# Three stages instead of four over the features of the first two token blocks, in a fused recurrence and cosine-gated feed-forward kernel

## The chip, the cores and the metric

The kernel runs on one core of a Trainium2 chip. The metric is the device time of one execution in microseconds (us). Before the change the median of three runs is 477.37 us (477.19 to 477.85). About 0.2% (0.95 us) is what a measurement of this kernel can tell from no change.

The engines are named as the profile names them: PE (TensorE, matmuls), PEld (its weight loads), DVE (VectorE), ACT (ScalarE), POOL (GpSimd) and SP (SyncE, whose queue issues nearly all DMAs).

## What is computed

```python
# r, k, v: (4, 8, 768, 48) float32; w, u: (8, 48)
for t in range(S):                       # a recurrence over 768 positions
    cur = einsum('bhd,bhe->bhde', u * k[t], v[t])
    y[t] = einsum('bhd,bhde->bhe', r[t], state + cur)
    state = w * state + einsum('bhd,bhe->bhde', k[t], v[t])
x = y.transpose(0, 2, 1, 3).reshape(3072, 384)
h = x @ w_in                             # w_in: (384, 2048), float64 in memory
out = ((h * cos(h)) @ w_out).astype(float32)   # w_out: (2048, 384), float64
```

## The kernel before, in words

**Attention.** The recurrence is computed in 24 chunks of 128 token rows. The first 8 (`chunk`, L1006) and the other 16 (`late_chunk`, `late_slot`, L1323 to L1633) use different loads and layouts, but each ends in a PSUM bank that holds 128 columns of x in three pieces of 128 features. ACT rounds that bank to the high half xh and DVE subtracts it to get the low half xl (L1233 and L1242 for the first 8 chunks, L1622 and L1627 in `split` for the late ones). For a late chunk the PSUM bank (`xp`) comes from the same ring of three banks (`B_H`) in which the feed-forward's products h are formed.

**Feed-forward.** The 24 chunks make six blocks of four chunks (512 token columns). The 2048 features are 16 groups of 128. One step is one block with one group: h takes 9 matmuls of 128x512 (three pieces of the 384 inputs times the three products high-high, low-high and high-low; `mm_h`, L553); then ACT and DVE take five passes over it (L571 whole turns, L574 the rest, L577 the sine table, L1733 the product with h, L1736 high half, L1739 low half); then 9 matmuls of 128x512 (`mm_ot`, L566) add the group's share to three accumulators in PSUM banks 0 to 2. The last block does its second product in the other orientation (`mm_o`, L559). PE is allowed to run the second product some steps after the first.

**Weights.** They lie in DRAM as float64. Each group has two pieces, one of w_in and one of w_out. A piece is loaded to a tile `raw` (ring of three, shared with the late chunks' loads), turned into float32 by integer operations (L934 on ACT, L942 and L954 on DVE, L963 an addition on POOL or DVE), rounded to a high half (L975 on ACT or L978 on DVE) and subtracted to a low half (L966 on DVE or POOL). `conv` (L906 to L983) writes these operations; the subtraction is `o8`. Of `conv(i)`, i = 2f is the w_in piece of group f and i = 2f+1 its w_out piece. They are converted once, and stay.

**Stages.** The weights come in slower than PE could use them if block 0 took all 16 groups first. So blocks 0 and 1 (`GRP = 2`) take turns: `CUTS` cuts the 16 groups into stages, block 0 takes a stage's groups, then block 1 takes the same ones, then the next stage begins. Blocks 2 to 5 take all groups in one go. With cuts at 0, 2, 5, 10 and 16 the 32 steps of the first two blocks need a new group at steps 0 and 1, 4 to 6, 10 to 14, and 20 to 25; in the steps between them block 1 uses groups that are there. At each turn the three accumulators are copied out of PSUM to an SBUF tile (L1787, the tile names are `ot`, `ztu` and `s`) and, when that block's next stage begins, copied back (L1766). All these copies run through two lambdas, L1760 on ACT and L1761 on DVE. The second products of the new stage wait for the copy back.

**The order.** Nothing runs in the order in which the program writes it. Each instruction group is an `Op` with an engine, a cost, a latency `lat` and a due time; `Plan.one_pass` (L427) is a list scheduler that picks, engine by engine, the operation that is ready with the earliest due time. It works with these numbers alone, before anything runs. The due times stand in the table `DUES` (one entry per operation, in nanoseconds), with `HOLDS` (how long an engine may be held for a more urgent operation) and `ALTS` (which of two engines an operation takes). `lat` is added to an operation's end both for the operations that depend on it and for the moment at which a buffer is free again:

```python
t = max(t, max(o.end + o.lat for o in x.owner.users))      # _free_at
t = max((d.end + d.lat for d in o.after), default=0.0)     # _ready
```

Once placed, each engine's queue is fixed: on the chip an engine waits at its next instruction even if a later one is ready. All first products are in the order of the steps (`line="h"`), and so are all second products (`line="o"`). Until the first h, PE's planned gaps are filled with dummy matmuls (`warm_up`, L1865).

Of the kernel before, what the change touches and what calls it, by code (L numbers as in the profile page):

```python
# [29 lines left out]
CUTS = (0, 2, 5, 10, 16)  # L30
# [285 lines left out]
}  # L316
ALTS = {
# [3 lines left out]
}  # L321
# [162 lines left out]
def kernel(  # L484
# [11 lines left out]
    nc = tc.nc  # L496
# [1526 lines left out]
```

## Time and profile before

| what | us |
|---|---|
| median of three runs | 477.37 |
| the profiled execution's own time | 478.65 |
| its span, first to last instruction | 476.8 |
| PE busy in the span | 468.6 (98%) |
| DVE busy | 366.2 (77%) |
| ACT busy | 303.1 (64%) |
| POOL busy | 212.8 (45%) |

The profiled execution's own time is 1.85 us longer than its span and 1.28 us longer than the median. TensorE's granted clock is 0.999 of full speed over the span. A view by windows gives the busy time of each engine in a stretch. A timeline row gives start, length, engine, line, operation, output and inputs; in brackets stands the idle time of that engine just before and what ended it. Matmul durations overlap: the pace of PE is read from the starts.

### The profile page before, as it was taken

What the parts mean: (1) busy time and instruction counts of PE and PEld (TensorE: products, weight loads), DVE (VectorE), ACT (ScalarE), POOL (GpSimd) and SP (SyncE); (2) the same over time, 40 slices, a digit from 0 to 9 for tenths busy, and PEclk for the clock granted to TensorE, in tenths of its full rate; (3) what the DMA queues carried; (4) which work ended last, traced back from release to release, by engine and by line L of the source; (5) the groups of instructions that cost most, each with busy time, mean ns of one, the idle gap of its engine ahead of it and who ended that gap; (6) DMA issues with size and microseconds to landing.
All of it is one profiled execution on the core that took longest, in us unless ns stands there. A gap on an engine that the chain in (4) does not pass through costs nothing.

```text
span 476.8 us, 11745 instructions
## 1 busy us (share of the span) xinstructions
PE 468.6 (98%) x4480; PEld 391.5 (82%) x4480; DVE 366.2 (77%) x679; ACT 303.1 (64%) x667; POOL 212.8 (45%) x217
## 2 busy tenths in 40 slices
PE   8899999999999999999999999999999999999996
PEld 7788888888878888788888888888888888898996
DVE  7998999999998877868887878776857666655552
ACT  5988978877877546465556556657547556344453
POOL 6865537536557786537864337543344200000000
PEclk9999999999999999999999999999999999999999
DMA  7883555437257646478646357644448300020001
GB/s 151 185 204 104 161 128 146 134 93 177 73 148 154 133 104 131 117 154 183 160 122 158 108 122 200 151 137 96 122 122 199 99 28 0 17 50 2 1 1 70
DMA packets 139233, 55.39 MB, mean 116 GB/s; under 512 B 122244, under 2 KB 135076, under 8 KB 139172
## 3 DMA queue, kind: packets, MB, share of 16 engines
q1 hardware_dynamic: 138964, 54.35, 47.0%
q8 instruction: 36, 0.59, 0.5%
q14 instruction: 25, 0.20, 0.1%
q10 hardware_dynamic: 208, 0.25, 0.1%
HBM read 49.86 MB, written 4.72 MB: 114 GB/s over the span
## 4 chain that ended last, share of the span: by engine, by line
PE 90%; DVE 3%; ACT 2%; POOL 2%; issue 1%; SPq 1%; DMA 1%; POOLq 0%; DVEq 0%
PE bank L553 39%; PE bank L566 33%; PE bank L559 7%; PE bank L1605 3%; PE bank L1521 3%; ACT A L1116 1%; PE bank L1143 1%; PE bank L1178 1%; DMA f<-in_r_dram 1%; PE bank L1212 0%; POOL A L1502 0%; PE bank L1051 0%; DVE f L574 0%; SPq L1374 0%; ACT qi L571 0%
## 5 line engine op out<-in xcount | busy, mean ns | idle before, releaser
L553 PE MATMUL bank<-xh,w_in_hi 128*128 128x512 f32 x288 | 112.7, 391 | 0.7 <-DVE xl L1627 0.7
L553 PE MATMUL bank<-xh,w_in_lo 128*128 128x512 f32 x288 | 112.4, 390 | 0.2 <-DVE w_in_lo L966 0.2
L553 PE MATMUL bank<-xl,w_in_hi 128*128 128x512 f32 x288 | 112.2, 390 | 0.0
L574 DVE SCALAR_TENSOR_TENSOR f<-bank,qi 128x512 f32<-128x512 f32 (+1 forms) x102 | 66.5, 654 | 46.1 <-ACT qi L571 45.9
L571 ACT ACTIVATE qi<-bank 128x512 int32<-128x512 f32 (+1 forms) x102 | 58.1, 574 | 64.3 <-PE bank L553 63.0
L566 PE MATMUL bank<-gh,w_out_hi 128*128 128x512 f32 x240 | 95.0, 396 | 0.0
L566 PE MATMUL bank<-gl,w_out_hi 128*128 128x512 f32 x240 | 93.5, 389 | 0.0
L566 PE MATMUL bank<-gh,w_out_lo 128*128 128x512 f32 x240 | 93.4, 389 | 0.0
L577 ACT ACTIVATE f<-f 128x512 f32<-128x512 f32 (+1 forms) x102 | 61.5, 607 | 36.6 <-DVE f L574 33.4
L1733 DVE TENSOR_TENSOR bank<-bank,f 128x512 f32<-128x512 f32 x94 | 64.9, 693 | 18.1 <-ACT f L577 16.4
L1736 ACT CAST gh<-bank 128x512 fp32r<-128x512 f32 x94 | 54.9, 585 | 36.8 <-PE bank L566 24.0
L1739 DVE TENSOR_TENSOR gl<-bank,gh 128x512 fp32r<-128x512 f32 x94 | 64.3, 684 | 15.8 <-ACT gh L1736 15.1
L553 PEld LDWEIGHTS bank<-xh,w_in_hi 128*128 128x128 f32 x288 | 54.1, 188 | 12.2 <-DVE xl L1627 1.1
L553 PEld LDWEIGHTS bank<-xh,w_in_lo 128*128 128x128 f32 x288 | 54.0, 188 | 11.9 <-DVE w_in_lo L966 0.6
L553 PEld LDWEIGHTS bank<-xl,w_in_hi 128*128 128x128 f32 x288 | 54.1, 188 | 10.9
L1460 POOL TENSOR_TENSOR A<-rT,decT_r 48x512 f32<-48x512 f32 x30 | 38.9, 1297 | 36.0 <-PE bank L1605 28.0
L566 PEld LDWEIGHTS bank<-gh,w_out_hi 128*128 128x128 f32 x240 | 45.0, 188 | 9.7
L566 PEld LDWEIGHTS bank<-gh,w_out_lo 128*128 128x128 f32 x240 | 45.0, 188 | 9.4
L566 PEld LDWEIGHTS bank<-gl,w_out_hi 128*128 128x128 f32 x240 | 45.1, 188 | 8.9
L963 POOL TENSOR_TENSOR f<-f,raw 128x384 int32<-128x384 int32 x24 | 26.1, 1090 | 40.6 <-DVE f L954 17.3
L1502 POOL TENSOR_TENSOR A<-ident,a 64x512 f32<-64x512 f32 x32 | 35.3, 1102 | 16.0 <-DVE a L1494 9.3
L1444 POOL TENSOR_TENSOR kT<-kT,decT_k 112x512 f32<-112x512 f32 x15 | 19.5, 1297 | 30.8 <-DVE kT L1429 25.5
(154 smaller groups left out, 726.2 us busy)
## 6 DMA issues: line engine op xcount, KB each, us to landing
raw<-in_moe_w_in_dram SPq DMA_DIRECT2D x29, 384.0 KB
raw<-in_moe_w_out_dram SPq DMA_DIRECT2D x29, 384.0 KB
raw<-in_k_dram SPq DMA_DIRECT2D x63, 80.0 KB
raw<-in_r_dram SPq DMA_DIRECT2D x63, 80.0 KB
out_dram<-ot SPq DMA_DIRECT2D x80, 48.0 KB
k<-in_k_dram SPq DMA_DIRECT2D x32, 96.0 KB
f<-in_r_dram SPq DMA_DIRECT2D x32, 96.0 KB
vr<-in_v_dram SPq DMA_DIRECT2D x32, 96.0 KB
```

Of the source, the lines that this page charges most:

```text
L553: nc.tensor.matmul(ph, a, b_, start=(i == 0), stop=(i == len(mm) - 1))
L559: nc.tensor.matmul(acc, a[:, ts], b_[:, f, :], start=(first and i == 0), stop=(last and i == 2))
L566: nc.tensor.matmul(acc, b_[:, f, n * P : (n + 1) * P], a, start=(first and i == 0), stop=(last and i == 2), skip_group_check=True)
L571: nc.scalar.activation(qi, ph, AF.Copy, scale=INV_2PI, bias=0.25)
L574: nc.vector.scalar_tensor_tensor(q, ph, INV_2PI, qi, op0=ALU.mult, op1=ALU.subtract)
L577: nc.scalar.activation(q, q, AF.Sin, scale=TWO_PI, bias=0.5 * math.pi)
L963: return lambda: eng.tensor_tensor(ai(), ai(), cn(), op=ALU.add)
L1460: nc.gpsimd.tensor_tensor(by_batch(plane(ar, j))[rows[j]], by_batch(late_t(rT))[rows[j]], late_d(decT_r)[rows[j]], op=ALU.mult)
L1502: nc.gpsimd.tensor_tensor(plane(ar, j)[side[j]], ident2[side[j], None, :].to_broadcast(to), ab()[side[j], :, None].to_broadcast(to), op=AL ...
L1733: nc.vector.tensor_tensor(g()[:, cs], ph()[:, cs], q()[:, cs], op=ALU.mult)
L1736: nc.scalar.copy(gh()[:, cs], g()[:, cs])
L1739: nc.vector.tensor_tensor(gl()[:, cs], g()[:, cs], f32(gh())[:, cs], op=ALU.subtract)
```

## The change

Blocks 0 and 1 take the groups in three stages of 2, 5 and 9 instead of four of 2, 3, 5 and 6. Two latencies that the scheduler reckons with are raised: that of a conversion's last subtraction, from 0.2 to 0.8 us for groups 8 to 15, and that of the late chunks' xl, from 0.2 to 1.0 us. All three tables are new.

```diff
-CUTS = (0, 2, 5, 10, 16)
+CUTS = (0, 2, 7, 16)
...
             o8 = op(
-                DVE, due - 0.8, 0.58, rest_of(nc.vector), [o7], [ca], port=True, alts=[(POOL, 1.15, rest_of(nc.gpsimd), True)]
+                DVE, due - 0.8, 0.58, rest_of(nc.vector), [o7], [ca], lat=0.2 if i < 16 else 0.8, port=True, alts=[(POOL, 1.15, rest_of(nc.gpsimd), True)]
             )
...
                     lambda: nc.vector.tensor_tensor(xo_(1), xv(), f32(xo_(0)), op=ALU.subtract),
                     [x_h],
                     [xp, xbuf],
+                    lat=1.0,
                 )
```

The cores of the tables: `DUES` has 2005 entries instead of 2017. Its first 56 entries (0 to 55, operations of the start-up and of the first chunks) are the same; from entry 56 on nearly all differ, in part because 12 operations are gone and the later ones move up. `HOLDS` has 1423 entries instead of 1220, and `ALTS` 33 in both:

```diff
-    26: 1, 44: 1, 132: 1, 137: 1, 143: 1, 156: 1, 615: 1, 629: 1, 636: 1, 641: 1, 648: 1, 657: 1, 676: 1, 677:
-    1, 685: 1, 690: 1, 720: 1, 740: 1, 741: 1, 753: 1, 767: 1, 783: 1, 788: 1, 804: 1, 811: 1, 823: 1, 825: 1,
-    869: 1, 915: 1, 941: 1, 999: 1, 2000: 1, 2010: 1,
+    26: 1, 44: 1, 132: 1, 137: 1, 143: 1, 156: 1, 615: 1, 629: 1, 636: 1, 641: 1, 648: 1, 657: 1, 684: 1, 690:
+    1, 720: 1, 747: 1, 748: 1, 762: 1, 767: 1, 781: 1, 788: 1, 790: 1, 797: 1, 802: 1, 810: 1, 811: 1, 825: 1,
+    869: 1, 939: 1, 981: 1, 1091: 1, 1993: 1, 1998: 1,
```

With cuts at 0, 2, 7 and 16 a new group is needed at steps 0 and 1, 4 to 8, and 14 to 22.

## Rows read from the trace of the kernel before

**Rows 1.** The page's head and its first part: busy time by engine.

```profile
span 476.8 us, 11745 instructions
PE 468.6 (98%) x4480; PEld 391.5 (82%) x4480; DVE 366.2 (77%) x679; ACT 303.1 (64%) x667; POOL 212.8 (45%) x217
```

**Rows 2.** Busy time by windows; the first row names the columns.

```profile
core 0: us, PE busy (x) PEld busy (x) DVE busy (x) ACT busy (x) POOL busy (x), PEclk, DMA share, GB/s
0.00:10.00 10.00, 8.59 (x79) 6.92 (x81) 6.57 (x24) 5.29 (x11) 6.34 (x24) 1.00 0.81 161
10.00:20.00 10.00, 8.76 (x160) 7.09 (x160) 9.58 (x18) 9.20 (x30) 9.04 (x10) 1.00 0.84 182
...
30.00:40.00 10.00, 9.43 (x216) 8.07 (x210) 9.30 (x19) 9.83 (x28) 6.76 (x8) 1.00 0.57 160
...
56.00:64.00 8.00, 8.00 (x37) 6.62 (x36) 7.13 (x15) 7.37 (x16) 4.39 (x4) 1.00 0.56 147
...
130.00:140.00 10.00, 9.85 (x44) 7.84 (x43) 9.71 (x20) 8.50 (x18) 4.47 (x4) 1.00 0.50 137
...
200.00:210.00 10.00, 9.32 (x42) 7.39 (x41) 6.27 (x10) 4.42 (x11) 6.72 (x6) 1.00 0.77 165
...
470.00:477.00 7.00, 2.69 (x16) 2.32 (x15) 0.42 (x2) 0.96 (x2) 0.00 (x0) 0.95 0.28 102
```

**Rows 3.** PE's timeline: its three waits after the first 20 us.

```profile
36.26 1.16 PE L1143 MATMUL bank<-rT,kT 48*128 48x128 f32 x16 [0.54 <-ACT kT L1093]
...
135.90 0.50 PE L553 MATMUL bank<-xh,w_in_lo 128*128 128x512 f32 x1 [0.15 <-DVE w_in_lo L966]
...
202.29 0.50 PE L553 MATMUL bank<-xh,w_in_hi 128*128 128x512 f32 x1 [0.68 <-DVE xl L1627]
```

**Rows 4.** Lines 1760 and 1761: accumulator copies, ns min/median/max.

```profile
L1760 ACT COPY bank<-ot x9: 580/596/622, 63.6 to 132.2; 128x512 f32<-128x512 f32 x9
...
L1761 DVE COPY s<-bank x2: 685/689/693, 63.7 to 87.0; 128x512 f32<-128x512 f32 x2
```

**Rows 5.** DVE's passes per step (busy us, mean ns) and per weight piece (min/median/max).

```profile
L1733 DVE TENSOR_TENSOR bank<-bank,f 128x512 f32<-128x512 f32 x94 | 64.9, 693 | 18.1 <-ACT f L577 16.4
L574 DVE SCALAR_TENSOR_TENSOR f<-bank,qi 128x512 f32<-128x512 f32 x94 | 64.5, 686 | 43.5 <-ACT qi L571 43.2
L1739 DVE TENSOR_TENSOR gl<-bank,gh 128x512 fp32r<-128x512 f32 x94 | 64.3, 684 | 15.8 <-ACT gh L1736 15.1
...
L942 DVE TENSOR_SCALAR f<-raw x32: 342/354/1219, 16.7 to 150.1; 128x384 int32<-128x384 int32 x32
...
L954 DVE SCALAR_TENSOR_TENSOR f<-raw,f x32: 532/551/1262, 20.4 to 151.2; 128x384 int32<-128x384 int32 x32
...
L966 DVE TENSOR_TENSOR w_in_lo<-f,w_in_hi x13: 517/551/1380, 25.5 to 142.8; 128x384 fp32r<-128x384 f32 x13
```

**Rows 6.** PE's timeline: first matmuls of steps 6, 7 and 8, and a second product.

```profile
60.09 0.39 PE L553 MATMUL bank<-xh,w_in_hi 128*128 128x512 f32 x1
...
62.13 0.39 PE L566 MATMUL bank<-gh,w_out_hi 128*128 128x512 f32 x1
...
64.17 0.39 PE L553 MATMUL bank<-xh,w_in_hi 128*128 128x512 f32 x1
...
70.29 0.39 PE L553 MATMUL bank<-xh,w_in_hi 128*128 128x512 f32 x1
```

**Rows 7.** DVE's and POOL's timelines, 58 to 70 us: conversions of groups 4 and 5.

```profile
58.16 0.55 DVE L966 TENSOR_TENSOR w_in_lo<-f,w_in_hi 128x384 fp32r<-128x384 f32 x1
...
65.89 0.70 DVE L1429 STREAM_TRANSPOSE kT<-raw 128x512 f32<-128x512 f32 x1
...
68.27 1.02 POOL L966 TENSOR_TENSOR w_out_lo<-f,w_out_hi 128x384 fp32r<-128x384 f32 x1 [0.29 <-ACT w_out_hi L975]
...
68.39 1.12 DVE L942 TENSOR_SCALAR f<-raw 128x384 int32<-128x384 int32 x1
69.43 0.55 DVE L966 TENSOR_TENSOR w_in_lo<-f,w_in_hi 128x384 fp32r<-128x384 f32 x1
```

548 rows, old and new, of tables (DUES, HOLDS) are left out of this document.

## The prediction, made before the result was known

> **What bounds the kernel now.** I read the page's busy times first, then the windows, then PE's waits. PE is busy 468.6 of 476.8 us [rows 1], so 8.2 us of the span are PE's idle time, and the windows say where they lie [rows 2]: 1.41 and 1.24 us in the first two stretches of 10 us, 0.57 between 30 and 40 us, 0.15 between 130 and 140, 0.68 between 200 and 210, and 4.1 after the last matmul (4.31 less the 0.2 by which that window overhangs the span). That makes 8.15; in every other stretch PE is never idle. The reader is to see two things. The kernel is bound by PE from 20 us to 472 us, so whatever frees DVE or ACT there gives nothing by itself. And the change has a ceiling: the number of matmuls stays the same (96 steps of nine for the first product, 80 of nine and 16 of twelve for the second), so all that it can win is PE's idle time. The 4.1 us at the end follow the last block, which it does not touch; the first 20 us are ordered by due times whose first 56 entries are the same. There remain three waits [rows 3]: 0.54 us at 36.26 for ACT's kT, 0.15 at 135.90 for a low half of w_in, 0.68 at 202.29 for xl. Ceiling: 1.4 us, 0.3% of the time.
>
> **What the removed copies are worth.** A stage boundary costs each of the two blocks three copies out and three back; four stages have three boundaries (36 copies), three have two (24). Twelve go, at 0.60 us on ACT or 0.69 on DVE [rows 4]: 12 x 0.60 = 7.2 us of engine time, nearly all ACT's. On PE's path I cost them at nothing: none of PE's three waits is for a copy [rows 3]. What hides them is that first products of later steps are queued ahead of the second product that needs the bank, 2.04 us each, as from 60.09 to 62.13 [rows 6]. Without that cover a boundary would show one copy out and one back in a row, 1.2 us, and two blocks lose one such boundary each: 2.4 us at most, of which the trace shows 0 now. The copies on DVE matter a little more, since DVE is the fuller engine, but only where it is late.
>
> **What the new stages ask for.** A step is 4.08 us of PE (64.17 less 60.09, nine matmuls of each product) [rows 6]. DVE's three passes take 0.69 + 0.69 + 0.68 = 2.06 us of it; a weight piece takes 0.354 + 0.551 + 0.551 = 1.46 us of DVE where POOL does the addition, so a new group with its two pieces 2.91 [rows 5]. A step with a new group thus asks 4.97 us of DVE and falls 0.89 behind PE; a step without one gains 4.08 - 2.06 = 2.02. Before, stage two is three such steps in a row; after, five. Before, w_in of group 5 is ready at 69.43 + 0.55 = 69.98 [rows 7], and its h starts at step 10. After, group 5 is needed at step 7, which starts at 64.17 [rows 6]: the conversion has to come 5.8 us sooner. Is there room? Group 4, the last one whose place does not move, is ready at 58.71 and needed at 60.09: 1.38 early [rows 6, 7]. Going on at 0.89 lost per step, group 5 would be 0.49 early, and group 6 0.40 late for step 8. One pass of that stretch is not due by then, the transpose of the first late chunk at 65.89 (0.70): putting it off leaves group 6 0.30 early. DVE also has 0.87 us idle between 56 and 64 [rows 2]. So the sum is: just in time, new wait 0. From the other side, if nothing can be moved forward, PE waits the whole 5.8 us. Between these ends I take 0, because the row of group 4's own conversion, which ends 1.38 before its use, is the nearest, but it is the step with the least margin, and the two values are far apart.
>
> In stage three nine groups follow each other: 9 x 0.89 = 8.0 behind, against 5 x 2.02 = 10.1 gained in block 1's five steps before them; before it was 6 x 0.89 = 5.3 against the same 10.1. The margin shrinks from 4.8 to 2.1 us, but what is left after step 22 is free of conversions for ten steps (before, step 25 and six), so that the late chunks' DVE work moves there. SP's queue and the ring of three raw tiles carry the same loads in another order. I cost this at 0 as well.
>
> **What the latencies are worth.** The wait at 202.29 is the ring of PSUM banks: an h may not overwrite the bank from which a late chunk's xl is still being subtracted. A latency of 1.0 instead of 0.2 makes the scheduler place that h at least 0.8 us later after xl, which is more than the 0.68 it waited; PE runs a second product in the gap. The wait at 135.90 is for a low half of a late group; 0.8 instead of 0.2 gives 0.6 against 0.15. Both should go: 0.83. What stands behind the postponed h on PE's queue is other matmuls that were due anyway. Bounds: 0 if something else is as late there, 0.83 if both go; I take 0.83, as each added margin exceeds the wait that its row shows. For the wait at 36.26 nothing in the change relieves ACT, busy 9.83 of 10 there [rows 2]; I leave it at 0, bounds 0 to 0.54, since only the new due times could move it.
>
> **Sum.** Against the profiled execution: 478.65 (span 476.8 and 1.85 around it) less 0.83 is 477.82. That execution lies 1.28 over the median; against the median, 477.37 - 0.83 = 476.5.
>
> **Rivals.** *Weights late (slower).* Place: step 8, group 6, about 68 to 70 us. What decides is whether DVE's instructions stretch by more than the 0.30 us of margin. At 68.39 a L942 took 1.12 us, where the median is 0.354, while POOL's subtraction ran from 68.27 to 69.29; it ended 0.22 after it [rows 5, 7]. So such a meeting costs 0.77. Four more pieces (two of group 5, two of group 6) now have to pass in this stretch; with one meeting each, 4 x 0.77 = 3.1, less 0.30, PE waits 2.8: 476.5 + 2.8 = 479.3. For it: the stretch is where DVE is fullest and POOL does part of the same conversions. Against: the median of 32 L942 is unstretched, so meetings are the exception. [...]
>
> *No change.* The two waits come from the chip running a little behind the plan, and new ones of the same size open at other places, since all due times are new: 477.4. For it: three different releasers in three waits, so no single cause. Against: the margins are raised at just the two operations of the larger waits in the feed-forward.
>
> *The whole ceiling.* The new order closes the wait at 36.26 too: 477.37 - 1.37 = 476.0. For it: the due times from entry 56 on cover the chunks that run there. Against: ACT is full.
>
> **How the numbers follow.** The forecast 476.5 gets 0.36, the whole ceiling 0.22, no change 0.20, late weights 0.22. Under 476.42 is faster by over 0.2%: all of the ceiling case and some 0.16 of the forecast, which lies on that edge, 0.38. Within 0.2%: the rest of the forecast and no change, 0.40. Slower by over 0.2%: 0.22. The range starts at 475.5, the ceiling case with half a microsecond for a start that shifts a little, and ends at 479.0, which takes in most of the late-weights case; left out are about 0.05 below and 0.13 above.
>
> **What would show it.** In the changed kernel's profile the waits of PE should no longer name xl or a low half of w_in after 100 us, the windows from 40 to 470 us should be full, and 24 copies should stand at lines 1760 and 1761's place. Late weights would show as PE waiting for w_in's low half, or its addition, between 60 and 75 us. I am wrong if the time moves by more than 1.4 us downwards: then the first 20 us or the end changed, which I hold to be fixed; or if PE waits for an accumulator's copy, which I costed at nothing.

## The result, and the profile after

The changed kernel takes 482.54 us (median of 4 runs, 482.22 to 482.98) against 477.61 for the one before beside it: 1.0104 times as long, interval 1.0091 to 1.0116. It is slower by 4.9 us, and outside the range that was stated (475.5 to 479.0). All times here are medians of several executions; a trace shows one. The executions of the kernel before lie between 477.0 and 479.4 us, and the one profiled for the prediction took 478.65.

The head of the changed kernel's page and its first part (line numbers are 20 higher than before for `mm_h`, `mm_ot` and `conv`, 21 for the passes of a step; L1781 is the accumulator copy on ACT):

```profile
span 480.4 us, 11735 instructions
PE 469.1 (98%) x4480; PEld 391.0 (81%) x4480; DVE 364.8 (76%) x681; ACT 297.5 (62%) x652; POOL 215.7 (45%) x218
```

Its waits of PE, by what was waited for (us in all, times, longest); those of the start-up are left out:

```profile
PE bank L573 <- ACT w_in_hi L995: 1.4, 1, 1.4
...
PE bank L586 <- ACT bank L1781: 1.0, 1, 1.0
PE bank L1163 <- ACT kT L1113: 0.9, 2, 0.5
PE bank L573 <- POOL w_in_lo L986: 0.6, 1, 0.6
...
PE bank L573 <- DVE w_in_lo L986: 0.3, 1, 0.3
```

The changed kernel's windows between 20 and 470 us that are not full, and 200 to 210 us (columns as in [rows 2]):

```profile
30.00:40.00 10.00, 9.06 (x203) 7.70 (x196) 9.49 (x21) 9.87 (x28) 6.63 (x9) 1.00 0.57 164
60.00:70.00 10.00, 9.02 (x41) 7.13 (x40) 8.78 (x19) 8.43 (x17) 4.71 (x5) 1.00 0.59 151
120.00:140.00 20.00, 17.73 (x189) 13.65 (x178) 19.22 (x37) 13.91 (x30) 9.24 (x9) 1.00 0.49 137
200.00:210.00 10.00, 10.00 (x164) 8.22 (x163) 9.14 (x19) 6.03 (x16) 8.05 (x7) 1.00 0.67 170
```

PE's busy time hardly changed (469.1 after 468.6 [rows 1]); its idle time did: 480.4 - 469.1 = 11.3 us after 8.2. The two waits in the feed-forward of [rows 3] are gone, and the window 200 to 210 is full. New are 0.98 us near 66 us and 2.27 us between 120 and 140. The four new waits in PE's timeline:

```profile
66.43 0.50 PE L586 MATMUL bank<-gh,w_out_hi 128*128 128x512 f32 x1 [0.98 <-ACT bank L1781]
...
124.17 0.50 PE L573 MATMUL bank<-xh,w_in_hi 128*128 128x512 f32 x1 [1.38 <-ACT w_in_hi L995]
...
125.17 0.50 PE L573 MATMUL bank<-xh,w_in_lo 128*128 128x512 f32 x1 [0.26 <-DVE w_in_lo L986]
...
130.17 0.50 PE L573 MATMUL bank<-xh,w_in_lo 128*128 128x512 f32 x1 [0.62 <-POOL w_in_lo L986]
```

124.17 is step 19, which needs group 12, and 130.17 step 20 with group 13: the middle of the nine-group stage. What stood ahead of group 12's conversion shows in the timelines of DVE, ACT and POOL:

```profile
112.64 2.68 POOL L1480 TENSOR_TENSOR A<-rT,decT_r 48x512 f32<-48x512 f32 x2
116.50 1.23 POOL L1505 TENSOR_TENSOR k<-k,dec_k 128x384 f32<-128x384 f32 x1
...
114.62 0.92 DVE L962 TENSOR_SCALAR f<-raw 128x384 int32<-128x384 int32 x1
116.76 1.19 DVE L962 TENSOR_SCALAR f<-raw 128x384 int32<-128x384 int32 x1
122.73 0.54 DVE L1647 TENSOR_TENSOR xl<-bank,xh 128x384 fp32r<-128x384 f32 x1
123.20 0.55 DVE L1598 TENSOR_TENSOR bank<-bank,zc 112x384 f32<-112x384 f32 x1
123.78 0.74 DVE L1573 COPY_PREDICATED A<-upper,bank 64x512 f32<-64x512 int32 x1
124.56 0.56 DVE L986 TENSOR_TENSOR w_in_lo<-f,w_in_hi 128x384 fp32r<-128x384 f32 x1
...
122.54 1.05 ACT L1588 COPY vr<-zc 48x384 f32<-48x384 f32 x2
123.61 0.51 ACT L995 CAST w_in_hi<-f 128x384 fp32r<-128x384 f32 x1
```

Work of late chunks (xl, state, mask on DVE; the copies vr on ACT) stands directly ahead of the two conversions (w_in_hi and w_in_lo) that PE waits for, and POOL's multiplications for another late chunk ran beside the integer passes. Two L962 took 0.92 and 1.19 us, where the median before was 0.354 [rows 5]; each ended 0.22 us after POOL's instruction (112.64 + 2.68 = 115.32 against 115.54; 117.73 against 117.95), the pattern of [rows 7]. What ties the two ends together is not shown. The two meetings cost DVE 0.57 + 0.84 = 1.4 us.

### The profile page after: what moved, and what is told of

Its sections match the earlier page's. It is cut to its first block, busy times and chain, and to the rows that moved or that the text cites. A ratio compares the mean times of both kernels' runs of the same rounds, so it can differ in the third digit from the quotient of the medians.

```text
span 480.4 us, 11735 instructions
## 1 busy us (share of the span) xinstructions
PE 469.1 (98%) x4480; PEld 391.0 (81%) x4480; DVE 364.8 (76%) x681; ACT 297.5 (62%) x652; POOL 215.7 (45%) x218
## 4 chain that ended last, share of the span: by engine, by line
PE 89%; DVE 4%; ACT 3%; issue 1%; POOL 1%; DVEq 0%; POOLq 0%; ACTq 0%
PE bank L573 40%; PE bank L586 32%; PE bank L579 7%; PE bank L1625 3%; PE bank L1541 3%; ACT A L1136 1%; PE bank L1163 1%; PE bank L1198 1%; DVE f L962 1%; DVE f L974 1%; PE bank L1071 0%; DVE f L594 0%; PE bank L1232 0%; ACT gh L1757 0%; ACT kT L1113 0%
## 5 line engine op out<-in xcount | busy, mean ns | idle before, releaser
L594 DVE SCALAR_TENSOR_TENSOR f<-bank,qi 128x512 f32<-128x512 f32 (+1 forms) x102 | 66.6, 656 | 55.8 <-ACT qi L591 53.3
L1480 POOL TENSOR_TENSOR A<-rT,decT_r 48x512 f32<-48x512 f32 x30 | 40.3, 1344 | 33.8 <-PE bank L1625 27.2
L983 POOL TENSOR_TENSOR f<-f,raw 128x384 int32<-128x384 int32 x25 | 27.1, 1086 | 41.8 <-DVE f L974 26.4
```

Of the source, the lines that this page charges most:

```text
L594: nc.vector.scalar_tensor_tensor(q, ph, INV_2PI, qi, op0=ALU.mult, op1=ALU.subtract)
L983: return lambda: eng.tensor_tensor(ai(), ai(), cn(), op=ALU.add)
L1480: nc.gpsimd.tensor_tensor(by_batch(plane(ar, j))[rows[j]], by_batch(late_t(rT))[rows[j]], late_d(decT_r)[rows[j]], op=ALU.mult)
```

## The experiments

The theories in question: **A**, up to step 22 the engines that feed PE owe more conversions than they can deliver, in whatever order; **B**, the amount of work is fine, and the order of the queues that came with the new tables is not; and, as a part of either, that POOL's instructions, running beside DVE's, stretch the conversions. The texts of e1 to e4 were written first and name theirs in their own words. "Thin" means that an instruction stays in its place in the queue and works on a small part of its data.

| run | us, median (lowest to highest) | ratio to before, interval |
|---|---|---|
| changed kernel | 482.54 (482.22 to 482.98) | 1.0104 (1.0091 to 1.0116) |
| e1 early groups | 484.89 (484.15 to 486.23) | 1.0149 (1.0132 to 1.0166) |
| e2 thin integer passes | 481.64 (481.34 to 482.40) | 1.0091 (1.0074 to 1.0108) |
| e3 thin late chunks, DVE | 482.79 (481.93 to 483.68) | 1.0111 (1.0092 to 1.0130) |
| e4 thin late chunks, POOL | 481.65 (481.42 to 482.31) | 1.0090 (1.0073 to 1.0107) |
| e10 all three thin | 481.56 (480.90 to 482.31) | 1.0080 (1.0065 to 1.0096) |
| e11 thin copies at group 2 | 481.82 (481.24 to 483.10) | 1.0098 (1.0081 to 1.0114) |
| e5 before, thin copies at group 5 | 477.20 (476.90 to 477.67) | 0.9992 (0.9982 to 1.0001) |
| e12 before, three places | 477.39 (477.08 to 478.07) | 1.0000 (0.9991 to 1.0009) |
| e15 group 12 ahead | 483.04 (482.50 to 483.59) | 1.0108 (1.0091 to 1.0125) |
| e16 groups 12, 13 ahead | 483.40 (482.99 to 483.71) | 1.0119 (1.0102 to 1.0136) |
| e9 conversions first | 480.39 (480.29 to 480.90) | 1.0064 (1.0050 to 1.0078) |
| e6 changed, other tables | 479.14 (477.94 to 480.79) | 1.0037 (1.0022 to 1.0051) |
| e7 stages alone, other tables | 481.09 (480.95 to 481.46) | 1.0075 (1.0061 to 1.0090) |
| e8 latencies alone, other tables | 479.65 (479.47 to 481.26) | 1.0044 (1.0031 to 1.0057) |
| e13 three stages, new order | 478.46 (477.32 to 479.98) | 1.0020 (1.0010 to 1.0030) |
| e14 four stages, new order | 478.43 (478.13 to 479.67) | 1.0025 (1.0015 to 1.0035) |

A trace shows one execution, and not always one at the median: those of e1, e8 and e10 lie 1.3, 1.6 and 0.75 us over their medians, those of e6 and e13 1.0 and 0.6 us under.

### Less work, same order (e1 to e4, e10)

All five keep every queue of the changed kernel. e1 lets PE use early weights:

```diff
+            fw = f - 7 if 14 <= s <= 22 else f      # used by h and o in place of f
```

> The changed kernel, but in block 0's third stage (steps 14 to 22) the matmuls read the weights of groups 0 to 8, which are there long before, instead of groups 7 to 15; the conversions still run, the order of every queue is the same. Theory A (the weights of the nine-group stage are late): PE's waits for w_in between 122 and 130 us, 2.27 us in the trace, go and nothing takes their place: 480.2 us. Theory B (the new order is worse by itself, and PE would be held up by the next thing behind the weights, such as gl or a PSUM bank): 482 us or more, with other releasers in the same stretch.

The weight waits went, yet it took 484.89 us: not A's 480.2. B's text (482 or more, with other releasers) is met, with a time 2.4 us above the changed kernel that it did not foresee. PE, no longer held at 124 us, ran into the passes of step 19, 2.11 and 0.36 us, about the 2.26 us that the three weight waits had been. PE's timeline of e1:

```profile
129.91 0.39 PE L573 MATMUL bank<-xh,w_in_lo 128*128 128x512 f32 x1
132.41 0.77 PE L586 MATMUL bank<-gh,w_out_hi 128*128 128x512 f32 x1 [2.11 <-ACT gh L1759]
133.54 0.80 PE L586 MATMUL bank<-gl,w_out_hi 128*128 128x512 f32 x1 [0.36 <-DVE gl L1762]
134.13 0.63 PE L586 MATMUL bank<-gh,w_out_lo 128*128 128x512 f32 x1
134.56 0.63 PE L586 MATMUL bank<-gh,w_out_hi 128*128 128x512 f32 x1
```

Between 120 and 130 us, where the changed kernel waited longest, e1 has no wait. So the weights were only the first thing that the queues delivered late. The passes were late by the queue too: DVE began its first pass over that step's h (L594) at 129.65 us, with no idle time before it, behind nine instructions on weight pieces that had kept it busy from 125.90 us on. (The clock's part is in the last section.) e2, e3 and e4 shorten one engine's work:

```diff
-                    ai(), hw(), 3, 0x3FFFFFF8, ...
+                    ai()[:, 0:nw], hw()[:, 0:nw], 3, 0x3FFFFFF8, ...     # e2; nw = 4 for f >= 7
...
-                    nc.vector.transpose(to, blocks)
+                    nc.vector.transpose(to[:, 0:ne], blocks[:, 0:ne])    # e3; ne = 1 for i < 10
...
-                nc.gpsimd.tensor_tensor(mb(), mb(), flat_u, op=ALU.mult)
+                nc.gpsimd.tensor_tensor(mb()[:, 0:nd], mb()[:, 0:nd], flat_u[:, 0:nd], op=ALU.mult)  # e4
```

> The changed kernel; DVE's two integer passes of the weight pieces of groups 7 to 15 work on 4 columns of 384, so that these groups' weights are not converted properly; order and buffers are the same. Theory A, with DVE as the engine that makes the weights late: 18 pieces x about 0.8 us less work, the waits at 122 to 130 us go, 480.2 us. [...] Theory B: 482.5 us.

> The changed kernel; DVE's transposes (two) and masks (two) of the late chunks 8 and 9 work on an eighth of their data, so that these chunks' x is not right; conversions and order are untouched. In the stretch 108 to 124.5 us this takes some 2 us of DVE's work from in front of group 12's conversion. Theory A, in the form that the late chunks' DVE work between the conversions is what the sum of the prediction left out: the waits at 122 to 130 us shrink from 2.27 to 0.5 us or less, 480.5 us. [...]

> The changed kernel; POOL's multiplications of the late chunks 8 and 9 (two decays of k, the decay of r, two bonus products) work on a small part of their data, so that these chunks' x is not right; DVE's own work and all orders are untouched. [...] Theory A with DVE's amount of work as cause: at most half a microsecond faster, 482 us.

e2 and e4 took the same 0.9 us off, and left the same waits: 0.7 us for w_in_hi and 0.4 for w_in_lo (e4 has 0.3 for gl besides). e2 (481.64) lies between the 480.2 and the 482.5 of its text; e4 (481.65) gains more than the half microsecond that its text allows if DVE's amount of work is the cause. POOL's work does take part: with it thin, DVE was busy for 43.69 us between 70 and 120 us, after 45.84 in the changed kernel, though none of its own instructions had less to do. e3 changed nothing (1.4, 0.7 and 0.5 us of waits). Unlike as the reliefs are, e2 and e4 stop at the same value, so a third thing may take over there. e10 put all three together.

> The changed kernel in its own order with the three reliefs at once: integer passes of groups 7 to 15 on 4 columns, the transposes and masks of late chunks 8 and 9 on an eighth, POOL's products of these chunks on a fraction. Each alone left 1.1 to 2.2 us of the 2.3 us of waiting near 124 and 130 us. If these waits are work queued ahead of the conversions on three engines together: they go altogether (0.3 us or less are left between 120 and 140 us), the 0.98 us at 66.4 us stays, 480.0 to 480.8. If something else sets them (the transfers of the weights, the order on ACT, which is thinned nowhere here): 481.5 or more, with w_in_hi waited for near 124 us.

481.56 us, and again 0.7 us for w_in_hi. The four executions lie in two pairs, 480.9 and 482.2 to 482.3 us, on both sides of what the text was to tell apart; the trace is of the longest. (In it 0.7 us lie elsewhere, in a longer wait for kT near 38 us, and PE runs 1.5 us later than in the changed kernel, as at a late chunk's product (L1633) at 121.16 instead of 119.71 us; so the wait is still 0.7 us though PE comes later. What the shorter pair waited for is not shown.) ACT and POOL in e10:

```profile
120.08 1.02 POOL L984 TENSOR_TENSOR f<-f,raw 128x384 int32<-128x384 int32 x1 [4.16 <-DVE f L975]
...
122.36 0.48 ACT L1650 CAST xh<-bank 128x384 fp32r<-128x384 f32 x1 [1.04 <-PE bank L1633]
...
123.26 1.05 ACT L1596 COPY vr<-zc 48x384 f32<-48x384 f32 x2
124.33 0.51 ACT L996 CAST w_in_hi<-f 128x384 fp32r<-128x384 f32 x1
```

The sum for group 12 was ready at 120.08 + 1.02 = 121.10. ACT stood idle for 1.04 us, waiting for PE's late-chunk product, because that chunk's xh is ahead in its queue (in the changed kernel it began xh at 121.63 us with no idle time before it); then came another piece and the copies vr; w_in_hi began 3.2 us after it could have. The wait here runs from PE through ACT's queue back to PE, and with shorter work on DVE and POOL together it still came to 0.7 us, as with either alone in e2 and e4: this speaks for B.

### The copies (e5, e11)

Both put the copies of one boundary on 4 of 512 columns: e5 in the kernel before at the boundary which the change removes, e11 in the changed kernel at the first boundary.

```diff
-                            (ACT, 0.55, lambda: nc.scalar.copy(dst(), src()), False),
+                            (ACT, 0.55, lambda: nc.scalar.copy(dst()[:, 0:nw], src()[:, 0:nw]), False),
...
+                        way, other = moves(acc[m], sums[n, m], 4 if f0 == 5 else TB)   # e11: f0 == 2
```

> The kernel before, every queue in its own order, with the twelve copies of the boundary that the change removes (six to the side after group 4, six back before group 5) on 4 of their 512 columns. The prediction costed these copies at 0: TensorE had no wait of 0.1 us at that boundary, so this kernel keeps the time of the one before, 477.5, within 0.2% (476.6 to 478.5). The rival, that a copy sets back every order behind it: 12 x 0.6 us of ACT and VectorE less let the waits of 0.15 and 0.68 us at 135.9 and 202.3 us go: 476.7. If the copies were dear (2.4 us, the prediction's upper bound), 475.

477.20 us, within 0.2%: no worth of the removed copies can be told, as predicted (the interval allows 0 to 0.9 us). This run also gives a trace of the old order in an execution near the median (its own time 476.98), with these copies thin. Its span is 475.3 us, PE is busy for 468.2 of it. PE's waits in e5, all that its profile names:

```profile
PE bank L1868 <- DVE wr L694: 1.2, 1, 1.2
PE bank L1178 <- DVE A L1151: 0.9, 1, 0.9
PE bank L1143 <- ACT kT L1093: 0.5, 1, 0.5
```

and one long window of it:

```profile
40.00:470.00 430.00, 430.00 (x3866) 360.48 (x3858) 329.48 (x600) 265.61 (x576) 183.87 (x171) 1.00 0.45 112
```

From 40 to 470 us PE is never idle: the waits of 0.15 and 0.68 us [rows 3] are not in this execution. The thin copies could have taken them away, as the text's rival has it; e12, below, has all copies whole.

> The changed kernel in its own order, with the copies of the boundary that both kernels have (six to the side after group 1, six back before group 2) on 4 of their 512 columns. The wait of 0.98 us at 66.4 us ended with such a copy. If it is the copies' own time (three aside and three back through one set of banks, 0.59 and 0.56 us each): the wait falls to 0.3 us or less and the time to 481.6 to 482.0. If it was only a symptom, and TensorE would find the weights of the next group (the low half of group 5 is ready at 68.5 us) as late: the 0.7 to 1 us come back at 69 to 70 us, and the time stays at 482.5.

481.82 us, and the wait at 66.4 us is gone (4.87 of 5 us busy between 65 and 70), while the later waits stay (1.4, 0.6 and 0.3 us). So the kept copies cost 0.7 us of the 4.9 by the medians, whose ranges overlap, and 0.98 us by the traces.

### One place, two places, a hundred (e15, e16, e9)

```diff
         order = plan.order()
+        for n, at in ((774, 241), (775, 241), (776, 242)):    # e16: and (790, 795)
+            order.remove(plan.ops[n])
+            order.insert(order.index(plan.ops[at]), plan.ops[n])
```

Operations 774 to 776 are the last three of group 12's w_in piece, 241 and 242 the late chunk's xh and xl, 790 the low half of group 13.

> The changed kernel with three instructions further ahead: the conversion of group 12 (POOL's addition, ACT's high half, VectorE's low half) goes ahead of the late chunk's xh, xl, state copy and mask. In the trace ACT's high half could then start at 122.1 instead of 123.61 us and the low half end at 123.3 instead of 125.1. If one badly placed conversion is at fault: the waits of 1.38 and 0.26 us go and the time falls by 1.6 us, to 480.9. If a row of conversions is late: TensorE comes 1.6 us sooner to step 20, whose low half still ends at 130.1 us, so the wait of 0.62 us there grows to some 2.2 us and the time stays within 0.5 us of 482.5.

> As the run before, and on POOL the low half of group 13 goes ahead of the addition of a later piece, which lay before it from 127.76 to 129.1 us. The low half could then run from 128.5 to 129.5 us, 0.6 us sooner, no more, since its integer passes wait for a transfer that ends at 126.8 us. If a row is late: 0.6 us less than the run before, some 481.9. If one place is at fault: no difference between the two, 480.9.

483.04 and 483.40 us. The wait was not removed but passed on. PE's waits in e15:

```profile
124.75 0.50 PE L573 MATMUL bank<-xh,w_in_lo 128*128 128x512 f32 x1 [0.55 <-DVE w_in_lo L986]
127.51 0.50 PE L586 MATMUL bank<-gh,w_out_lo 128*128 128x512 f32 x1 [0.42 <-DVE w_out_lo L986]
129.99 0.50 PE L573 MATMUL bank<-xh,w_in_hi 128*128 128x512 f32 x1 [0.60 <-ACT w_in_hi L995]
131.56 0.50 PE L573 MATMUL bank<-xh,w_in_lo 128*128 128x512 f32 x1 [0.83 <-POOL w_in_lo L986]
```

In all 2.40 us, after 2.26 in the changed kernel, now spread over w_in and w_out of group 12 and both halves of group 13; e16 has 2.18 us in five waits. (PE was late already before the first of these waits: the late chunk's product L1625 began at 120.67 us in e15 and at 120.07 in e16, after 119.71 in the changed kernel.) A whole row of conversions is late, and one mended place only brings PE sooner to the next. e16's 0.6 us did not come either.

e9 keeps PE's order and moves 108 instructions of the other queues (DVE, ACT, POOL and SP, which issues the loads), all between 55 and 145 us:

```diff
+        order[282:750] = [plan.ops[n] for n in ORDER]     # conversions of groups 8 to 15 ahead of late chunks' masks, products, state
```

> The changed kernel, TensorE's order and every instruction as they are; between some 55 and 145 us 108 instructions stand elsewhere in the queues of VectorE, ACT, POOL and SyncE: the conversions of groups 8 to 15 go ahead of the masks, the state's copies and the products of the late chunks 9 and 10, which come 10 to 20 us later. Theory B (it is the order of these queues, not the amount of work, that makes stage three late): the waits of 1.38, 0.26 and 0.62 us between 124 and 131 us shrink to 0.7 us or less in all, the wait of 0.98 us at 66.4 us stays, and the time is 480.3 to 481.2. Theory A (too little of the three engines before step 22, whatever the order): the waits come back under other names, as they did when the weights were taken from earlier groups, and the time is 482 to 484.

480.39 us, 2.1 us under the changed kernel, as B expected. Its windows:

```profile
100.00:120.00 20.00, 19.27 (x85) 15.63 (x85) 19.18 (x35) 14.52 (x31) 13.84 (x14) 1.00 0.66 163
120.00:140.00 20.00, 19.80 (x205) 15.88 (x204) 18.38 (x37) 14.95 (x31) 8.03 (x8) 1.00 0.47 133
```

2.27 us of idle time between 120 and 140 became 0.20, no instruction shorter or left out; 0.73 us came back at 119 us as a wait for gl. Over the whole span PE's idle time fell by 1.3 us (11.3 to 10.0) and its busy time by 0.6 (469.1 to 468.5).

### Stages and latencies with other orders (e6 to e8, e13, e14)

In e6, e7 and e8 only the tables differ from the changed kernel (e6), from the kernel before with the new cuts (e7) and with the new latencies (e8); e13 and e14 have the queues of e6 and of the kernel before in a further order.

> The changed kernel (three stages, both latencies) with another table of due times, and so another order on every queue; no instruction is added or left out. Theory A (before step 22 the engines that feed TensorE owe more conversions than they can deliver, whatever the order): the two long waits can be spread and cut, but 1 to 2 us of waiting stay in 120 to 140 us, and the time is 478.5 to 480.5, not under the kernel before. Theory B (the order that the new tables give is all that is wrong): no wait over 0.3 us in 120 to 140 us and the time of the kernel before or less, 476 to 477.5.

> The kernel before with the three stages alone (both latencies as before) and an order of its own. If the latencies cost or bring nothing, as much as the changed kernel with another order, within 0.3%; theory A: 478.5 to 480.5 with a wait of 0.5 us or more between 120 and 140 us. If the longer latencies are what makes the third stage late, this one is at or under 477.5.

> The kernel before (four stages) with the two latencies alone and an order of its own. Theory A: the four stages leave room, no wait over 0.3 us in 120 to 140 us; the waits of 0.15 us at 135.9 and 0.68 us at 202.3 go and the time is 475.5 to 476.8, faster than both kernels. Theory B (any new order costs as much as the changed kernel's): 480 or more. If the latencies bring nothing: 477.0 to 478.

e6 took 479.14 us. A's time, but not A's waits: in its profiled execution (478.16, span 476.3) PE has no wait between 100 and 200 us. e7 took 481.09, over its text's numbers, with other waits (kT 0.8, k 0.5, xl 0.5 us). e8, four stages, took 479.65, none of its text's numbers; its profiled execution, of 481.26 us, has 1.6 us of waiting for gl: 1.34 us of PE's idle time lie between 200 and 210 us, where the old order's wait for xl had been. An order of its own cost every variant 1.7 to 3.6 us, the four stages too. So e7 against e6 does not separate the latencies from the order, and these three runs left the stages' own sign open. e13 and e14 compare three stages with four, with orders searched alike.

> Three stages, as in the run of the changed kernel with another order (e6), with 340 of its 2005 instruction groups at other places in their queues (TensorE's included), searched so that the order holds at several lengths of the conversions and of the hand-overs. Theory B (the order alone cost the changed kernel its 5 us): no wait over 0.4 us after 50 us, and 475.5 to 477.0. Theory A (the nine-group stage needs more of the feeding engines than they have): one or more waits of 0.5 us or more between 60 and 140 us and 478 or more.

> Four stages, the kernel before with its own tables and 342 instruction groups at other places, searched in the same way. If the prediction's ceiling of 1.4 us is all that order or stages can bring: 476.0 to 477.0, within 0.5 us of the run with three stages, whichever is first. If three stages save what their 12 copies cost: this one is slower than the run with three stages by 0.5 us or more. If three stages cost cover in stage three: this one is faster by 0.5 us or more.

478.46 and 478.43 us: equal, both 0.2% over the kernel before, and neither at or under the 477.0 that the texts named for a good order. PE's waits in e13, all that its profile names:

```profile
PE bank L1968 <- DVE wr L793: 1.2, 1, 1.2
PE bank L1277 <- DVE A L1250: 0.8, 1, 0.8
PE bank L1242 <- ACT kT L1192: 0.2, 1, 0.2
```

and e13's windows in stage three:

```profile
120.00:130.00 10.00, 10.00 (x46) 8.27 (x45) 9.97 (x20) 6.99 (x15) 3.38 (x3) 1.00 0.51 161
130.00:140.00 10.00, 10.00 (x46) 8.29 (x45) 8.07 (x15) 6.56 (x14) 6.21 (x7) 1.00 0.54 120
```

Nine new groups in a row, PE full: A has fallen. With as good an order, three stages cost nothing and bring nothing that these runs can tell. Both lie 0.9 us over the kernel before, and their traces (477.88 and 478.43 us, spans 476.1 and 476.6) show no waiting that would explain it: PE idles for 6.7 and 7.2 us, in e5 and e12 for 7.1 and 7.4, but it is busy for 469.4 us in both, after 468.2 and 468.0, with the same 4480 matmuls. Why the same matmuls take longer in the new orders is open, and the executions up to 479.98 have no trace.

### The old waits taken away (e12)

```diff
+        for n, at in ((342, 343), (790, 800), (158, 831)):    # xl, w_in_lo and kT ahead; then as in e15
```

> The kernel before with four stages, its tables and latencies, and three instructions one to three places further ahead in their queue: the late chunk's xl ahead of a mask on VectorE (TensorE waited 0.68 us for it at 202.3 us), w_in_lo of group 14 ahead of an integer pass (0.15 us at 135.9 us), and the copy of kT ahead of gh and ztu on ACT (0.54 us at 36.3 us). If a wait of TensorE is worth its length where nothing else is late behind it: 1.2 to 1.4 us less, 476.1 to 476.4, faster than both kernels. If the next operand is as late (gl behind the mask, or gh behind kT): 477.0 to 477.6.

477.39 us, no difference (the interval is 0.4 us to either side, so 0.83 us would have shown). The waits at 135.9 and 202.3 us are gone from its profile, with none new after 40 us; that for kT stands (0.64 us, at 37.9 us). Taken with e5: the 0.83 us that the prediction meant to win were waits of the one profiled execution, not of the median. This is inferred, since the kernel before has no trace at its median.

No version of either kind was found that beats the kernel before. A further raw tile for the late chunks, which would take their loads out of the weights' ring, was not tried. That the ring of raw tiles makes some conversions late is therefore not excluded: in the changed kernel ACT waits 0.38 and 0.41 us for transfers of weights, at 125.88 and 126.86 us.

## Why the prediction was wrong

**The ceiling and what it was held against.** That PE bounds the kernel, that its busy time would about stay (469.1 after 468.6; it is not quite fixed, as the 469.4 of e13 and e14 show), and that the removed copies are worth nothing that can be told (e5) was right. The sum then took 0.83 us of waits out of the execution of 478.65 us and subtracted them from the median, 477.37. Its own text had the warning: that execution lay 1.28 us over the median. In e5, near the median, the two waits do not occur, and with both taken away the median stays (e12). This step of the sum failed: the term measures 0 in place of 0.83, and by e5's trace the ceiling for the median was not 1.4 but the wait for kT, 0.5 us.

**Stage three.** "The margin shrinks from 4.8 to 2.1 us ... so that the late chunks' DVE work moves there ... I cost this at 0": this is the step that failed most. The count of DVE's time was not wrong (e13 runs nine groups without a wait). But the count says what an order could do, and the step took for granted that the new tables do it. They left the late chunks' xh, xl, mask, state and products ahead of group 12's and 13's conversions: 2.27 us. By places alone e9 leaves 0.20 us there and 0.73 just before, and takes 2.1 us off the median. That these are the only places that matter is not shown: e9 moved 108 instructions at once, and moving three or four (e15, e16) brought nothing.

**Stage two and the copies.** Step 8, named as the one with least margin, had no wait. But the conversion came too late for the cover: w_in of group 5 was ready at 69.05 us instead of the 0.49 us ahead of step 7 at 64.17 that was reckoned, and step 7 began at 69.28. No first product stood between the last second products of block 1's turn and the first of block 0's, and PE met the row of copies:

```profile
65.06 0.39 PE L586 MATMUL bank<-gh,w_out_lo 128*128 128x512 f32 x1
66.43 0.50 PE L586 MATMUL bank<-gh,w_out_hi 128*128 128x512 f32 x1 [0.98 <-ACT bank L1781]
...
69.28 0.39 PE L573 MATMUL bank<-xh,w_in_hi 128*128 128x512 f32 x1
...
65.29 0.59 ACT L1781 COPY s<-bank 128x512 f32<-128x512 f32 x1
65.76 1.12 ACT L1781 COPY bank<-ot 128x512 f32<-128x512 f32 x2
...
68.50 0.55 DVE L986 TENSOR_TENSOR w_in_lo<-f,w_in_hi 128x384 fp32r<-128x384 f32 x1
```

One copy out and one back in a row, 0.98 us: the prediction had this price (1.2 us "without that cover") and did not connect it with the lateness of group 5 that it discussed next. A wait for an accumulator's copy was one of the two things that it named as showing it wrong.

**The rivals.** *Weights late* had the right mechanism and sign, with 0.22, but the wrong stage, and a price from meetings with POOL's instructions alone. POOL's work took part (e4: 0.9 us), but e2 takes off as much, and in e10's trace the wait for w_in_hi stands (0.7 us) with both reliefs. That the new due times might simply be a worse order than the old ones was mentioned under *no change*, with new waits "of the same size". They were larger.

**The balance.** Between the traces of e5 and of the changed kernel: after 40 us the old order has no idle time before 470 us; the changed one has 0.98 + 2.27 = 3.25. Between 30 and 40 us it has 0.94 after 0.57 [rows 2]. These 3.6 us and 0.9 more of busy time (469.1 after 468.2 in e5's trace) make 4.5 of the 5.1 us between the spans of 480.4 and 475.3; the rest lies in the first 20 us (2.85 us idle after 2.24), and there the changed kernel's own order has 2.29 in e11's execution.

## What to carry to other kernels

A change to a kernel with a fixed, searched order is two changes: the structure and a new order; price the second by asking, for each queue, what stands ahead of the operand with the least margin, and compare the structures only with orders made alike. Count idle time that is to be won against an execution at the median, or look for it in a second trace. If halving the work of one engine after the other leaves the same wait, look for a queue in which the wanted instruction stands behind one that waits for the engine that waits, as w_in_hi in e10 began 3.2 us after its input was ready.

## What the runs showed of the hardware that was not expected

In e1 PE, never idle between 120 and 130 us, stood idle for 2.11 us, and its granted clock fell: the windows from 133 to 139 us show 0.50, after 1.00 up to 132 us. The matmuls of the timeline above then start 0.43 us apart (134.13, 134.56) instead of 0.23, until 139.25 us; from 134.13 to 138.83 eleven of them lose 0.20 each, 2.2 us, and with those at the edges the fall costs some 3 us, more than the wait itself. The trace is of the longest of e1's executions (486.23 us). Its span is 4.0 us over that of the changed kernel's trace: 3.3 us of it are PE's busy time (472.4 after 469.1), which is where the fall shows, and 0.7 us idle time (12.0 after 11.3), as much as the wait for kT is longer (1.7 after 0.9). Whether the clock fell as much in the other three executions is not shown; their mean granted clocks are 0.992 to 0.996. The changed kernel's longest wait there, 1.38 us, left the clock at 1.00. Windows of e1, PE alone (length, busy, count, granted clock, DMA):

```profile
132.00:133.00 1.00, 0.59 (x1) 0.73 0.89 247
133.00:134.00 1.00, 0.64 (x2) 0.50 0.43 169
...
138.00:139.00 1.00, 1.00 (x4) 0.50 0.65 143
```
